# Second layer's X of blocks 1 to 4 transposed by VectorE instead of TensorE, with the orders of an opening, a late head pair and the last slots altered

## The chip, the cores and the metric

One Trainium2 chip, of which the kernel uses one core. The metric is the time of one execution in microseconds (us) of device time, as the median of several runs. A profile of one execution gives the span from its first to its last instruction, the instructions of each engine and the transfers of the DMA queues.

## The reference, cut to what matters

Three stages in fp32, one feeding the next. The shapes are fixed.

```
q, k, v : (4, 8, 576, 64)    f : (4, 8, 576)
attn = softmax(q k^T / 8 + decay(f), causal) v      # 32 heads, 576 tokens each
x = attn as (2304, 512)                             # tokens x model width

logits = x w_gate + modality_bias[modality_id]      # 8 experts, top 1
for each expert e:                                  # w1[e] 512 x 1024, w2[e] 1024 x 512
    y[tokens of e] = gate * (relu(x w1[e]) w2[e])

h = y w_in                                          # "second layer": 512 x 2048
out = max(0.01 h, h) w_out                          # 2048 x 512
```

## The kernel before, in words

TensorE is the engine that nearly everything goes through. Each fp32 product is made of three products of fp32r halves (high x high, high x low, low x high), so every operand is split by ScalarE (high half) and VectorE (low half) ahead of its matmuls.

**Attention** (0 to about 205 us) goes over 16 pairs of heads, g = 0 to 15. Its order on all five engines is written out by hand (`ordered(tc, MS)`): `first(g)`, `last(g)`, `third(g)`, `fourth(g)`. The operands of a pair are made ahead of it. `load(g)` brings the raw q and k (576 KB, 64 partitions of q over 64 of k). `prep_hi(g)`, called in `fourth(g - 2)`, makes the high half `aq` on VectorE (L386), brings three small row sets from `agd` (L390, L391) and copies the high half of k from partitions 64 to 127 to `bk` by a DMA (L393). `prep_lo(g)`, called in `first(g - 1)`, makes the low half (L403) and moves three more half tiles between partitions by DMAs (`bq`, `ak`, and `aq` onto itself at L406, which may start only when the copy at L393 has read its source). All these DMAs are issued by SyncE (SP), whose instructions go in order, and run on one queue. In `fourth(g)` the order before is `load(g + 3)`, `vload(g + 1)`, `prep_hi(g + 2)`.

The first pair has its q and k loaded twice, onto both partition halves (`qk0`), so that it needs no copies between partitions; pair 1 goes through `load`, `prep_hi`, `prep_lo` like the rest. Matmuls of no use, `warm(n)`, fill TensorE's first waits.

**Experts** (about 205 to 459 us). The tokens are put in slots of 128, each of one expert. `step(t)` runs slot t: first product `gemm1`, transposes `trh`, second product `gemm2` of the slot before, splits of the weights of the next slot (`split`), and the output `yout`, which scales by the gate (ScalarE, L1091) and scatters the rows to `yd` in DRAM (GpSimd). 18 steps always run; each further one stands in a branch on the number of slots (20 steps run with these inputs), and after the last comes `tail`, which ends the last slot and transposes X of block 0. Order by hand on all engines in `step`, on three in `tail`.

**Second layer** (about 459 us to the end). The 2304 tokens are cut into five blocks, four of 512 and one of 256. For each group of four of the 16 hidden blocks fb, and each token block b, `visit` runs `g1(b, fb)`: 12 matmuls into `u`, whose result goes ScalarE, VectorE, ScalarE, VectorE (L1303 to L1307) into the halves `gh`, `gl`; and `g2` of the visit before: 12 matmuls per 512 tokens. X of block b + 1 has to stand in SBUF, transposed to 128 features x 4 x 512 tokens in two halves, before `g1(b + 1, 0)`. `xload(b + 1)` is called at the first visit of block b and brings four tiles of 128 tokens (rows of 2052 bytes, the last word being the token's number). `xts` transposes a tile by four TensorE transposes into PSUM (L989), from which ScalarE makes the high and VectorE the low half (L993, L994). GpSimd copies the token numbers to `tid` (L985). Up to the first visit of block 1 TensorE's order is that of the program; after it the scheduler orders all engines by a simulated timeline. SP's first load of block 1 has to wait until the last scatter to `yd` has landed.

Of the kernel before, what the change touches and what calls it, by code (L numbers as in the profile page):

```python
# [19 lines left out]
P = 128  # L20
# [56 lines left out]
def fused(ctx: ExitStack, tc, qk0, qk2, vp, f, mid, wg, mb, w1, w2, w_in, w_out, out):  # L77
# [146 lines left out]
    with tc.tile_pool(name="pst", bufs=PST, space=PSUM) as pst:  # L224
# [15 lines left out]
        def gload(i):  # L240
            if i == 0:
                nc.sync.dma_start(wgs, wg.rearrange("(k p) e -> p k e", p=P))
                return
            nc.sync.dma_start(mbs.rearrange("p m e -> p (m e)"), mb.rearrange("(o m) e -> o (m e)", o=1).broadcast_to([P, 2 * E]))
            m32 = mid.bitcast(I32)
            for b in range(B):
                t0 = b * S
                nc.sync.dma_start(midi[:, b * NC:b * NC + 4, :], m32[t0:t0 + 4 * P, :].rearrange("(c p) t -> p c t", p=P))
            nc.sync.dma_start(midi[:64].rearrange("p (b c) t -> p b c t", c=NC)[:, :, 4, :], m32.rearrange("(b s) t -> s b t", b=B)[4 * P:])
# [23 lines left out]
        def load(g):  # L273
            if g == 1:

                xt[0] = pe.tile([P, NC, XW], F32, tag="x", name="x0")
                raw = xt[0].rearrange("p c d -> p (c d)")[:, :2 * S].rearrange("p (h s) -> p h s", h=2)
            else:
                raw = pe.tile([P, 2, S], F32, tag="raw", name=f"raw{g}", bufs=3)
            nc.sync.dma_start(raw, qk2[:, 2 * g:2 * g + 2, :])  # L280
            ops[g] = raw
# [21 lines left out]
        def start():  # L303
# [11 lines left out]
            load(1)  # L315
# [34 lines left out]
            load(2)  # L350
# [27 lines left out]
            nc.gpsimd.memset(midi, 0)  # L378
            ops[0] = (aq, bq, ak, bk)

        def prep_hi(g):
# [3 lines left out]
            bq, bk, a4, b4 = bqs[g % NBUF], bks[g % NBUF], aq4[g % NBUF], bq4[g % NBUF]  # L385
            nc.vector.tensor_scalar(aq, raw, qs, None, ALU.mult)  # L386
            if g == 1:
                nc.sync.dma_start(bk[0:64].bitcast(F32), h[64:128])
            for t, r0, c0 in ((bq, 64, 0), (bk, 66, 2)):
                nc.sync.dma_start(t[r0:r0 + 2].bitcast(F32), agd[c0:c0 + 2, 2 * g:2 * g + 2, :])  # L390
            nc.sync.dma_start(b4[64:66, :, :64].bitcast(F32), agd[0:2, 2 * g:2 * g + 2, 4 * P:])  # L391
            if g > 1:
                nc.sync.dma_start(bk[0:64].bitcast(F32), h[64:128])  # L393
# [526 lines left out]
        with ordered(tc, MS):  # L920
            start()
            prep_hi(1)
# [39 lines left out]
    xp = ctx.enter_context(tc.tile_pool(name="xp", bufs=4))  # L962
# [14 lines left out]
    def xts(b, sb, psums, part=None):  # L977
# [4 lines left out]
        for i in range(n // P) if part is None else part:  # L982
            r = XR[b, i]
            if t0 < FIX:
                nc.gpsimd.tensor_copy(tid[:, t0 // P + i:t0 // P + i + 1], r[:, DM:].bitcast(I32))  # L985
# [6 lines left out]
            c = slice(i * P, (i + 1) * P)  # L992
# [54 lines left out]
    with tc.tile_pool(name="rt2", reuse_waits="tile", bufs=1) as rt2, \  # L1047
# [16 lines left out]

        def keepg(t):
# [12 lines left out]
        def gemm2(t, k0, k1):  # L1078
            if k0 == 0:
# [345 lines left out]
```

## Time and profile before

| | |
|---|---|
| median of 3 runs | 864.98 us (864.28 to 865.23) |
| time of the profiled execution | 865.08 us |
| its span, first to last instruction | 863.4 us |
| TensorE busy, share of the span | 853.7 us, 99% |
| VectorE, ScalarE, GpSimd busy | 589.8, 503.3, 198.1 us |
| mean granted clock of TensorE | 0.996 of full speed |

The busy time of an engine is the sum of what its instructions cover. With one engine at 99%, a saving counts where that engine's work is removed or where it waits; what the other engines do counts where TensorE would have to wait for it. Times in the trace are us from the span's start.

### The profile page before, as it was taken

To read this page: it belongs to the slowest core of one execution; us is meant where nothing else is said; L and a number is where in the kernel's file an instruction comes from. 1 tells how busy PE (TensorE), PEld (TensorE's weight loads), DVE (VectorE), ACT (ScalarE), POOL (GpSimd) and SP (SyncE) were. 2 spreads that over 40 slices of the span, in tenths; PEclk is the share of its full clock that TensorE was granted. 3 is DMA by queue.
4 is the path that set the end of the run, shared out by engine and by line. 5 is a ranking of instruction groups with operands and counts; after the bars stand their busy time and mean duration, and the time that the engine had idled before them with its cause. 6 is when DMAs were issued, how large, how long until landed. Compare 5 with 4: busy or idle time off the path is not lost.

```text
span 863.4 us, 14450 instructions
## 1 busy us (share of the span) xinstructions
PE 853.7 (99%) x4760; PEld 705.9 (82%) x4760; DVE 589.8 (68%) x983; ACT 503.3 (58%) x965; POOL 198.1 (23%) x305
## 2 busy tenths in 40 slices
PE   8999999999999999999999999999999999999998
PEld 5888888878888888888878888888888888888887
DVE  6688777777769999999975563386337943473334
ACT  5888878867368999999884544353223422242222
POOL 6102222341148354339721000000000000001111
PEclk8999999999999999999999999999999999999999
DMA  7676787886485154131223240042001300011111
GB/s 224 174 192 178 206 216 195 208 204 227 113 284 185 63 168 155 40 97 62 81 83 89 64 132 0 1 126 70 1 0 51 122 25 1 0 49 49 50 49 74
DMA packets 34359, 92.96 MB, mean 108 GB/s; under 512 B 8582, under 2 KB 9254, under 8 KB 34275
## 3 DMA queue, kind: packets, MB, share of 16 engines
q1 hardware_dynamic: 29618, 77.23, 31.8%
q0 software_dynamic: 4640, 14.71, 5.2%
q8 instruction: 40, 0.66, 0.3%
q14 instruction: 45, 0.36, 0.1%
q10 hardware_dynamic: 16, 0.00, 0.0%
HBM read 132.09 MB, written 14.99 MB: 170 GB/s over the span
## 4 chain that ended last, share of the span: by engine, by line
PE 94%; DMA 2%; ACT 1%; DVE 1%; issue 1%; DVEq 0%; ACTq 0%; SPq 0%
PE u L1301 23%; PE a L1321 23%; PE h L215 13%; PE y L1083 13%; PE pv L527 5%; PE pt L515 4%; PE sc L426 2%; PE sc L427 2%; PE th L1073 2%; PE xo L551 1%; DMA bk<-aq 1%; PE tx L203 1%; PE pt L505 1%; PE sc L480 1%; PE sc L478 1%; PE fx L989 1%
## 5 line engine op out<-in xcount | busy, mean ns | idle before, releaser
L1303 ACT COPY us<-u 128x512 f32<-128x512 f32 (+1 forms) x80 | 43.4, 543 | 165.4 <-PE u L1301 165.1
L1304 DVE SCALAR_TENSOR_TENSOR us<-u,us 128x512 f32<-128x512 f32 (+1 forms) x80 | 51.0, 637 | 125.7 <-ACT us L1303 125.2
L1301 PE MATMUL u<-fxl,whii 128*128 128x512 f32 (+1 forms) x320 | 117.6, 369 | 0.0
L1301 PE MATMUL u<-fxh,whii 128*128 128x512 f32 (+1 forms) x320 | 117.5, 370 | 0.0
L1301 PE MATMUL u<-fxh,wloi 128*128 128x512 f32 (+1 forms) x320 | 117.5, 369 | 0.0
L1321 PE MATMUL a<-whio,gh 128*128 128x512 f32 x280 | 109.5, 391 | 0.0
L1321 PE MATMUL a<-wloo,gh 128*128 128x512 f32 x280 | 109.3, 390 | 0.0
L1321 PE MATMUL a<-whio,gl 128*128 128x512 f32 x280 | 104.7, 389 | 0.0
L177 DVE TENSOR_TENSOR w1l<-w1r,w1h 128x1024 fp32r<-128x1024 f32 x72 | 87.2, 1235 | 11.6 <-ACT w1h L173 11.6
L1334 POOL DMA_INDIRECT out<-acc,tid x16 | 15.8, 986 | 336.0 <-DVE acc L1328 299.1
L177 DVE TENSOR_TENSOR w2l<-w2r,w2h 128x1024 fp32r<-128x1024 f32 x68 | 80.2, 1222 | 1.3 <-ACT w2h L173 1.1
L441 ACT ACTIVATE p<-sc,nm 128x128 f32<-128x128 f32 (+3 forms) x128 | 66.1, 526 | 22.2 <-DVE nm L436 20.2
L1306 ACT CAST gh<-us 128x512 fp32r<-128x512 f32 (+1 forms) x76 | 44.6, 587 | 52.6 <-DVE us L1304 43.4
L173 ACT CAST w1h<-w1r 128x1024 fp32r<-128x1024 f32 x72 | 73.8, 1055 | 0.8 <-PE h L215 0.8
L1307 DVE TENSOR_TENSOR gl<-us,gh 128x512 fp32r<-128x512 f32 (+1 forms) x76 | 49.3, 648 | 36.1 <-ACT gh L1306 35.5
L173 ACT CAST w2h<-w2r 128x1024 fp32r<-128x1024 f32 x68 | 69.5, 1052 | 2.4 <-PE y L1083 2.0
L436 DVE TENSOR_REDUCE nm<-sc 128x2 f32<-128x256 f32 (+1 forms) x64 | 51.1, 820 | 27.1 <-PE sc L432 21.0
L1301 PEld LDWEIGHTS u<-fxh,wloi 128*128 128x128 f32 x320 | 60.3, 188 | 10.4
L1301 PEld LDWEIGHTS u<-fxh,whii 128*128 128x128 f32 x320 | 60.3, 188 | 10.1
L1301 PEld LDWEIGHTS u<-fxl,whii 128*128 128x128 f32 x320 | 60.3, 188 | 10.1
L166 POOL DMA_INDIRECT xg<-xs,gidx x22 | 58.5, 2657 | 36.9 <-PE xo L551 13.2
L1083 PE MATMUL y<-w2h,hh 128*128 128x512 f32 x160 | 64.6, 404 | 1.2 <-ACT hh L1075 1.2
(337 smaller groups left out, 1871.5 us busy)
## 6 DMA issues: line engine op xcount, KB each, us to landing
w1r<-w SPq DMA_DIRECT2D x88, 512.0 KB
w2r<-w SPq DMA_DIRECT2D x82, 512.0 KB
rwi<-w_in SPq DMA_DIRECT2D x16, 512.0 KB
rwo<-w_out SPq DMA_DIRECT2D x16, 512.0 KB
raw<-qk SPq DMA_DIRECT2D x14, 576.0 KB
vt<-vp SPq DMA_DIRECT2D x16, 320.0 KB
xr<-yd SPq DMA_DIRECT2D x18, 256.5 KB
bk<-aq SPq DMA_DIRECT2D x15, 288.0 KB
```

Source lines behind the costliest of these rows:

```text
L166: nc.gpsimd.indirect_dma_start(out=xg[t % 2], out_offset=None, in_=xs[:n, :], in_offset=bass.IndirectOffsetOnAxis(ap=m[:, i:i + 1], axis=0 ...
L173: nc.scalar.copy(hi, raw)
L177: nc.vector.tensor_tensor(lo, raw, hi.bitcast(F32), ALU.subtract)
L215: nc.tensor.matmul(Hp[t][:, n, :], lhsT=xp[t % 2][:, k * P:(k + 1) * P], rhs=wp[k][:, n * 512:(n + 1) * 512], start=(k == 0 and i == 0), s ...
L436: nc.vector.tensor_reduce(nm, view, axis=AX.X, op=ALU.max, negate=True)
L441: st["exp"] = nc.scalar.activation(pt[:, j, :], view[:, j, :], AF.Exp, bias=nm[:, j:j + 1], scale=1.0, accum_out=sms[g % 3][:, c, j:j + 1])
L1083: nc.tensor.matmul(Yp[t], lhsT=ap[:, k * P:(k + 1) * P], rhs=wp[k // 2][:, k % 2, :], start=(k == 0 and i == 0), stop=(k == NFB - 1 and i ...
L1301: nc.tensor.matmul(ps, lhsT=w[:, k * P:(k + 1) * P], rhs=x[:, k, :], start=(i == 0), stop=(i == 3 * NKB - 1))
L1304: nc.vector.scalar_tensor_tensor(us, ps, 0.01, us, ALU.mult, ALU.max)
L1306: nc.scalar.copy(gh, us)
L1307: nc.vector.tensor_sub(gl, us, gh.bitcast(F32))
L1321: nc.tensor.matmul(A[b][i], lhsT=x[:, c], rhs=w, start=(first and m == 0), stop=(last and m == 2))
```

## The change

1. **X of blocks 1 to 4.** `xload` brings a block with four DMAs, one for each quarter of the features, of 32 partitions each: partition 32 j + i holds, for quarter j, the tokens i, 32 + i, 64 + i, ..., in pieces of 512 bytes. One VectorE transpose in 32x32 blocks for each tile of 128 tokens (128x512 fp32, read in steps of 16 bytes) then gives the tile with features on the partitions; ScalarE and VectorE split it from SBUF. TensorE has no part in it. The order of the features becomes 4 p + k for partition p, which the host's layout of `w_in` follows; block 0, still on TensorE, reads its tile in steps of 16 bytes for that. All four tiles are in one buffer. The token numbers come by a DMA of their own. The tiles of blocks 2 to 4 move from visits 0, 0, 1, 2 to visits 2, 2, 3, 3 of the block before, ahead of `g1` in the program.
2. **Late pair.** In `fourth(g)`, `load(g + 3)` comes after `vload(g + 1)` and `prep_hi(g + 2)`.
3. **Opening.** Pair 1 is loaded like pair 0, onto both halves, k first, q in the place of `load(2)`. Its operands are made by `second(0)` to `second(2)` with one copy between partitions instead of four. `warm(4)` is put before the first transposes. `wgs` and `midi` are laid out on the host and come by one DMA each.
4. **Slots.** From slot 17 on, `yout(t - 2)` runs at the start of `step(t)` (or `tail`) instead of `yout(t - 1)` at the end, and `split(t, 0, 3)` at the start of `step(t)` instead of in `step(t - 1)`. The second product has one fixed PSUM tile.

```diff
 def load(g):
-    if g == 1:
-        xt[0] = pe.tile([P, NC, XW], F32, tag="x", name="x0")
-        raw = xt[0]...[:, :2 * S]
 def start():
-            load(1)
+            xt[0] = pe.tile([P, NC, XW], F32, tag="x", name="x0")
+            qr1, kr1 = (...[:, i * 2 * S:(i + 1) * 2 * S] ... for i in range(2))
+            nc.sync.dma_start(kr1, qk0[:, 1, 2:4, :])
...
-            load(2)
+            nc.sync.dma_start(qr1, qk0[:, 0, 2:4, :])
+def second(step):
+    if not step:
+        ...
+        nc.scalar.copy(ak, kr1)
+        nc.sync.dma_start(bks[1][0:64].bitcast(F32), ak[0:64].bitcast(F32))
+        operand_rows(1)
+        nc.vector.tensor_sub(ak[64:128], kr1[64:128], ak[64:128].bitcast(F32))
+        ...
+    if step == 1:
+        nc.vector.tensor_scalar(aq, qr1, 0.125, None, ALU.mult)
+        for r in (0, 64):
+            nc.gpsimd.tensor_copy(aq4[1][r:r + 64, :, :64], aq[0:64, :, 4 * P:].bitcast(F32))
+        return
+    nc.vector.scalar_tensor_tensor(bqs[1][0:64], qr1[0:64], 0.125, aq[0:64].bitcast(F32), ALU.mult, ALU.subtract)
+    nc.gpsimd.tensor_copy(bq4[1][0:64, :, :64], bqs[1][0:64, :, 4 * P:].bitcast(F32))
 def first(g):
-            if g + 1 < NG:
+            if 0 < g < NG - 1:
                 prep_lo(g + 1)
+            if not g:
+                second(1)
 def third(g):
+            if not g:
+                second(2)
...
+            if not g:
+                warm(4)
 def fourth(g):
-            if g + 3 < NG:
-                load(g + 3)
             if g + 1 < NG:
                 vload(g + 1)
             if g + 2 < NG:
                 prep_hi(g + 2)
+            if g + 3 < NG:
+                load(g + 3)
...
             start()
-            prep_hi(1)
+            second(0)
+            load(2)
 def xload(b):
-        for i in range(n // P):
-            XR[b, i] = xp.tile([P, XW], F32, tag="xr", name=f"xr{b}_{i}")
-            nc.sync.dma_start(XR[b, i], yd[t0 + i * P:t0 + (i + 1) * P, :])
+        r = xp.tile([P, 4, XW], F32, tag="xr", name=f"xr{b}")          # block 0: as before, in slices of r
+        XR[b] = r.rearrange("p c d -> p (c d)")[:, :n * 4]
+        for j in range(4):
+            nc.sync.dma_start(XR[b][32 * j:32 * j + 32].rearrange("b (q c) -> b q c", c=P), yd[t0:t0 + n, j * P:(j + 1) * P].rearrange("(q b) c -> b q c", b=32))
+        if t0 < FIX:
+            nc.sync.dma_start(tid[...].unsqueeze(2), yd[t0:t0 + n, DM:]...)
 def xts(b, sb, psums, part=None):
+            if b:
+                t = XQ[0].tile([P, 512], F32, tag="xq", name=f"xq{b}_{i}")
+                nc.vector.transpose(t.rearrange("p (i k c) -> p i k c", i=4, k=NKB), XR[b][:, i * 512:(i + 1) * 512].rearrange("p (i c k) -> p i k c", i=4, k=NKB))
+                t = t.rearrange("p (i k c) -> p k i c", i=4, c=32)
+                ...
+                nc.scalar.copy(h, t)
+                nc.vector.tensor_sub(l, t, h.bitcast(F32))
+                continue
+            rk = r[:, :DM].rearrange("p (c k) -> p k c", k=NKB)
             for k in range(NKB):
-                nc.tensor.transpose(ps[:, k * P:(k + 1) * P], r[:, k * P:(k + 1) * P], ident)
+                nc.tensor.transpose(ps[:, k * P:(k + 1) * P], rk[:, k], ident)
+        LATE = NSTAT - 1
 def tail(t):
+                if t >= LATE:
+                    yout(t - 1)
                 trh(t)
 def step(t):
+            if t > LATE:
+                yout(t - 2)
...
             keepg(t)
+            if t > LATE:
+                split(t, 0, 3)
...
-            if nx and t:
+            if nx and 0 < t < LATE:
                 split(t + 1, 0, 3)
...
-            if t:
+            if 0 < t < LATE:
                 yout(t - 1)
 def visit(v):
-                for k, i in (((2, 0), (2, 1), (3, 2), (3, 3)) if b == 0 else ((0, 0), (0, 1), (1, 2), (2, 3))):
+                for k, i in ((2, 0), (2, 1), (3, 2), (3, 3)):
...
-            for i in sorted(parts)[:1 if v <= GS else 2]:
+            for i in sorted(parts):
                 parts.pop(i)()
 host:
-    wi = ...reshape(NKB, P, NGB, P).transpose(1, 2, 0, 3)...
+    wi = ...reshape(P, NKB, NGB, P).transpose(0, 2, 1, 3)...
```

## Rows read from the trace of the kernel before

**Rows 1.** The page's first part: engine, busy us, share of the span, instructions.

```profile
PE 853.7 (99%) x4760; PEld 705.9 (82%) x4760; DVE 589.8 (68%) x983; ACT 503.3 (58%) x965; POOL 198.1 (23%) x305
```

**Rows 2.** Waits of TensorE: instruction waiting, releaser, us in total, times, longest.

```profile
PE sc L426 <- DMA aq<-aq: 1.6, 1, 1.6
PE y L1083 <- ACT hh L1075: 1.2, 1, 1.2
...
PE pt L515 <- ACT p L441: 0.8, 1, 0.8
PE sc L426 <- DVE ak L358: 0.8, 1, 0.8
```

**Rows 3.** Groups of TensorE by line, 467 to 535 us: the transposes of X.

```profile
L989 PE MATMUL fx<-ident,xr 128*128 128x128 f32 x56 | 8.4, 272 | 0.0
```

**Rows 4.** Chain that ended last, 440 to 560 us: start, us, what.

```profile
467.58 0.44 PE fx L989 x4
...
480.90 5.95 PE u L1301 x26
...
534.78 0.44 PE fx L989 x4
```

**Rows 5.** Groups of VectorE by line and shape: count, busy us, mean ns.

```profile
L1304 DVE SCALAR_TENSOR_TENSOR us<-u,us 128x512 f32<-128x512 f32 x64 | 44.2, 691 | 113.7 <-ACT us L1303 113.4
...
L675 DVE TENSOR_REDUCE lgs<-lp 128x40 f32<-128x320 f32 x1 | 0.8, 787 | 0.1
...
L754 DVE TENSOR_REDUCE stk<-ustk 128x20 f32<-128x160 f32 x1 | 0.3, 320 | 0.0
```

**Rows 6.** Timeline of SP's queue, 463 to 468 us: loads of block 1.

```profile
464.59 1.81 SPq L970 DMA_DIRECT2D xr<-yd  x4
```

**Rows 7.** Timeline of GpSimd, 463 to 468 us: first reader of those loads.

```profile
467.38 0.20 POOL L985 COPY tid<-xr 128x1 int32<-128x1 int32 x1 [5.44 <-DMA xr<-yd]
```

**Rows 8.** Windows: length, busy by engine, clock, DMA share, GB/s (last column).

```profile
15.60:17.00 1.40, 1.40 (x7) 1.40 (x7) 0.00 (x0) 1.40 (x6) 0.48 (x2) 0.50 1.06 204
...
466.00:470.40 4.40, 4.40 (x22) 3.51 (x21) 1.54 (x3) 1.21 (x2) 0.75 (x4) 1.00 0.92 285
...
480.90:505.10 24.20, 24.20 (x115) 19.96 (x115) 16.61 (x29) 13.46 (x23) 2.23 (x4) 1.00 0.38 108
```

**Rows 9.** Chain that ended last, 156 to 176 us.

```profile
161.43 9.20 DMA bk<-aq
...
170.68 3.54 DMA aq<-aq
```

**Rows 10.** Windows of the same stretch, columns as above.

```profile
159.00:170.00 11.00, 11.00 (x101) 9.38 (x100) 9.58 (x23) 9.14 (x28) 4.35 (x12) 1.00 0.97 212
...
170.50:171.50 1.00, 1.00 (x11) 0.88 (x10) 0.47 (x1) 0.31 (x2) 0.84 (x5) 1.00 0.18 60
```

**Rows 11.** Chain that ended last, 445 to 461 us.

```profile
447.85 1.76 ACT w2h L173 x2
...
449.63 0.70 ACT ys L1091
450.33 1.70 issue
...
452.16 0.59 ACT hh L1075
```

**Rows 12.** Windows of the opening, columns as above (PEclk is the third last).

```profile
13.00:14.00 1.00, 0.19 (x1) 0.18 (x1) 1.00 (x2) 0.70 (x4) 0.94 (x3) 0.88 0.96 207
14.00:20.60 6.60, 6.60 (x26) 5.14 (x26) 2.78 (x4) 3.89 (x15) 2.02 (x7) 0.50 0.81 172
```

**Rows 13.** Timeline of VectorE, 10 to 14 us.

```profile
10.93 0.82 DVE L386 TENSOR_SCALAR aq<-x,qs 128x1152 fp32r<-128x1152 f32 x1
12.16 1.02 DVE L436 TENSOR_REDUCE nm<-sc 128x2 f32<-128x256 f32 x2 [0.41 <-PE sc L429]
13.10 1.41 DVE L403 SCALAR_TENSOR_TENSOR x<-x,qs,aq 128x1152 fp32r<-128x1152 f32 x1
```

More of the change, by code (lines that the diff above doesn't have):

```diff
@@ L273, in load @@
         def load(g):
[L274 to L279 removed]
+            raw = pe.tile([P, 2, S], F32, tag="raw", name=f"raw{g}", bufs=3)
             nc.sync.dma_start(raw, qk2[:, 2 * g:2 * g + 2, :])
@@ L377, in start, with operand_rows @@
                 nc.gpsimd.memset(t[:, S:], 0.0)
-            nc.gpsimd.memset(midi, 0)
             ops[0] = (aq, bq, ak, bk)
+            ops[1] = (qr1, kr1)
+        def second(step):
+            if not step:
+                qr1, kr1 = ops[1]
+                aq, ak = (aqk.tile([P, 2, S], F32R, tag=n, name=f"{n}1") for n in ("aq", "ak"))
+                nc.scalar.copy(ak, kr1)
+                nc.sync.dma_start(bks[1][0:64].bitcast(F32), ak[0:64].bitcast(F32))
+                operand_rows(1)
+                nc.vector.tensor_sub(ak[64:128], kr1[64:128], ak[64:128].bitcast(F32))
+                st["second"] = qr1, aq
+                ops[1] = (aq, bqs[1], ak, bks[1])
+                return
+            qr1, aq = st["second"]
+            if step == 1:
+                nc.vector.tensor_scalar(aq, qr1, 0.125, None, ALU.mult)
+                for r in (0, 64):
+                    nc.gpsimd.tensor_copy(aq4[1][r:r + 64, :, :64], aq[0:64, :, 4 * P:].bitcast(F32))
+                return
+            nc.vector.scalar_tensor_tensor(bqs[1][0:64], qr1[0:64], 0.125, aq[0:64].bitcast(F32), ALU.mult, ALU.subtract)
+            nc.gpsimd.tensor_copy(bq4[1][0:64, :, :64], bqs[1][0:64, :, 4 * P:].bitcast(F32))
+        def operand_rows(g):
+            for t, r0, c0 in ((bqs[g % NBUF], 64, 0), (bks[g % NBUF], 66, 2)):
+                nc.sync.dma_start(t[r0:r0 + 2].bitcast(F32), agd[c0:c0 + 2, 2 * g:2 * g + 2, :])
+            nc.sync.dma_start(bq4[g % NBUF][64:66, :, :64].bitcast(F32), agd[0:2, 2 * g:2 * g + 2, 4 * P:])
         def prep_hi(g):
@@ L384, in prep_hi @@
             h = aq.bitcast(F32)
-            bq, bk, a4, b4 = bqs[g % NBUF], bks[g % NBUF], aq4[g % NBUF], bq4[g % NBUF]
+            bk, a4 = bks[g % NBUF], aq4[g % NBUF]
             nc.vector.tensor_scalar(aq, raw, qs, None, ALU.mult)
[L387 to L393, printed above, removed]
+            operand_rows(g)
+            nc.sync.dma_start(bk[0:64].bitcast(F32), h[64:128])
             for r in (0, 64):
@@ L967, in xload @@
         t0, n = blocks[b]
-        for i in range(n // P):
-            XR[b, i] = xp.tile([P, XW], F32, tag="xr", name=f"xr{b}_{i}")
-            nc.sync.dma_start(XR[b, i], yd[t0 + i * P:t0 + (i + 1) * P, :])
+        r = xp.tile([P, 4, XW], F32, tag="xr", name=f"xr{b}")
+        if not b:
+            for i in range(n // P):
+                XR[b, i] = r[:, i, :]
+                nc.sync.dma_start(XR[b, i], yd[t0 + i * P:t0 + (i + 1) * P, :])
+            return
+        XR[b] = r.rearrange("p c d -> p (c d)")[:, :n * 4]
+        for j in range(4):
+            nc.sync.dma_start(XR[b][32 * j:32 * j + 32].rearrange("b (q c) -> b q c", c=P), yd[t0:t0 + n, j * P:(j + 1) * P].rearrange("(q b) c -> b q c", b=32))
+        if t0 < FIX:
+            nc.sync.dma_start(tid[:, t0 // P:(t0 + n) // P].unsqueeze(2), yd[t0:t0 + n, DM:].bitcast(I32).rearrange("(c p) o -> p c o", p=P))
     X = {}
@@ L1063, in fused @@
         gc = mw.tile([P, 2], F32, name="gc")
+        yp = pmy.tile([P, 512], F32, name="yp")
         def keepg(t):
@@ L1078, in gemm2 @@
         def gemm2(t, k0, k1):
-            if k0 == 0:
-                Yp[t] = pmy.tile([P, 512], F32, tag="y", name=f"y{t}")
             for k in range(k0, k1):
                 for i, (ap, wp) in enumerate(((hh, w2h), (hh, w2l), (hl, w2h))):
-                    nc.tensor.matmul(Yp[t], lhsT=ap[:, k * P:(k + 1) * P], rhs=wp[k // 2][:, k % 2, :], start=(k == 0 and i == 0), stop=(k == NFB - 1 and i == 2))
-        Yp = {}
+                    nc.tensor.matmul(yp, lhsT=ap[:, k * P:(k + 1) * P], rhs=wp[k // 2][:, k % 2, :], start=(k == 0 and i == 0), stop=(k == NFB - 1 and i == 2))
         def yout(t):
@@ L1281, in fused @@
          tc.tile_pool(name="fz", reuse_waits="tile", bufs=1) as fz, \
+         tc.tile_pool(name="xq", reuse_waits="tile", bufs=2) as xq, \
          tc.tile_pool(name="pfa", reuse_waits="tile", bufs=1, space=PSUM) as pfa, \
@@ L1286, in fused @@
             wset(fx, i)
+        XQ.append(xq)
         G = {}
@@ L1400 @@
     w2 = inputs["moe_w2"].reshape(E, NFB, P, DM).transpose(0, 2, 1, 3).reshape(E, P, NFB * DM)
-    wi = inputs["moe2_w_in"].reshape(NKB, P, NGB, P).transpose(1, 2, 0, 3).reshape(P, NGB, NKB * P)
+    wi = inputs["moe2_w_in"].reshape(P, NKB, NGB, P).transpose(0, 2, 1, 3).reshape(P, NGB, NKB * P)
     arrays = {
-        "qk0": np.stack([np.concatenate([t, t], axis=0) for t in (qk2[:D, :2], qk2[D:, :2])], axis=1),
+        "qk0": np.stack([np.concatenate([t, t], axis=0) for t in (qk2[:D, :4], qk2[D:, :4])], axis=1),
         "qk2": qk2,
```

24 lines of the change are left out of this document (11 added, 13 removed).

## The prediction

> **What bounds the kernel now.** I read the page's first part first: TensorE is busy for 853.7 of 863.4 us [rows 1], so a gain has to be TensorE work removed or a TensorE wait closed, and a loss a new TensorE wait. Its list of waits holds four that the change touches, 4.4 us together: 1.6 for a copy of `aq`, 1.2 for `hh`, 0.8 for `p`, 0.8 for `ak` [rows 2]. The reader should see that the waits are few and single (each occurs once). Then I took the groups of TensorE in the stretch of the X transposes (56 of them, four for each of 14 tiles) [rows 3], the chain there for what a tile costs [rows 4], VectorE's groups for the price of the new work [rows 5], the queues that feed it [rows 6, 7] with windows for rates and load [rows 8], and one view for each wait [rows 9 to 13]. A difference within 0.2% (1.7 us) counts as no change: about what a measurement of this kernel can tell.
>
> **The sum's base.** The profiled execution took 865.08 us (span 863.4, 1.7 around it), 0.1 above the median of the runs shown. I sum against 865.1 and take 0.1 off at the end.
>
> **X, what leaves TensorE.** A row of four transposes takes 0.44 us of the chain [rows 4], the first and the last of 14, though each is listed with 272 ns [rows 3], since they overlap. 14 x 0.44 = 6.1 us. TensorE waits for nothing there and the transposes lie between its products, so all of it comes off: -6.1.
>
> **X, what VectorE gets.** 14 transposes of 128x512 fp32. No transpose by VectorE is in the trace. An operation of the same size that reads in sequence takes 0.69 us L1304 in [rows 5]. The change reads with a step of 16 bytes. The nearest row is the reduction L675, whose reads are 32 or 64 bytes apart: 320 elements in 787 ns, while the reduction L754 does 160 neighbouring ones in 320 ns. With about 153 ns fixed (691 less 512 at 1.05; 320 less 160 at 1.04 gives the same), L675 pays 1.98 ns an element, nearly double. So a transpose lies between 0.69 and 512 x 1.98 + 153 = 1.17 us; I take 1.17, the row with spread reads being nearest.
>
> The Trainium skill (SBUF — State Buffer, section Door 1: The DMA port swizzle) says that reads which change to another 16-byte line at every access pay for it, with no figure; by that the 0.69 is out, and the sum with 0.69 would be about 2 us lower. L675 agrees at 32 bytes, no row shows 16.
>
> **Block 1, the place where time goes back.** Its load starts when the last scatter has landed, at 464.6 [rows 6]. Before, the first tile (256.5 KB) had a reader at 467.38 [rows 7], 2.8 us later; at 285 GB/s [rows 8], 466.0 to 470.4 0.9 of that is transfer, 1.9 fixed. A VectorE transpose needs all four DMAs, since each brings 32 of the 128 partitions: 1.05 MB, 3.7 us at 285 GB/s, 5.1 at 204, the rate while copies to 64 partitions run [rows 8], 15.6 to 17.0. With so few partitions at a time I take 5.1: the data is there at 471.6 (470.2 at best). VectorE, in order, then has four transposes (4.7), four low halves at 0.69 (2.8), and between them three steps of visits 2 and 3 (2.1): 9.5 us, so X stands at 481.1. TensorE needs it for u(1,0), now at 480.9 [rows 4], but five groups of 0.44 vanish ahead of it: 478.7. A wait of 2.4 us, on an engine that had none. Behind it stand g2(0,3) and all after. Best: loads at 470.2 and transposes at 0.69 (7.6 us) end at 477.8, no wait. Worst: the two further VectorE steps of those visits are ordered ahead too and one more 0.7 is lost to waiting for ScalarE's high halves: +4.5. I take +2.4.
>
> **Blocks 2 to 4.** Here the load has a visit or more to spare: one buffer means that it waits for the transposes of the block before, but it is issued about 20 us ahead of need. What is tight is VectorE while block 1 is multiplied, when weights 4 and 5 of the second layer are split too: 16.6 busy of 24.2 us [rows 8], 480.9 to 505.1. Four transposes add 4.7, the stretch loses 1.8: 21.3 of 22.4. It fits, barely; +0.5, between 0 and +2.4 (half of what is added turns up as waits). The token DMA (512 words per block) and GpSimd's 12 copies less are hidden: GpSimd is busy 23% [rows 1], and the numbers are needed at the output. On SP's queue only weight loads stand behind the new five DMAs per block, not needed until the second group of hidden blocks.
>
> **Late pair.** The chain: copy of `bk` 9.2 us, then `aq` 3.54, then TensorE [rows 9]. The queue ran at 0.97 share until 170, so the copy of `bk` was long because the load of pair 15 (576 KB) and others stood in front of it. With the load behind, `bk` lands 590 KB / 212 GB/s = 2.8 us earlier, and the copy of `aq`, which waits for it on SP, is issued earlier. The bytes ahead of `aq` are the same either way, so only the hole counts: 0.18 share from 170.5 to 171.5 and the ramp around it [rows 10], some 1.5 us. The move puts a vload and prep_hi's four DMAs ahead of the load on SP; the load then also waits for VectorE's `aq`, with only the low-half copies and stores behind it, and is needed a pair later. So 1.5 of the 1.6 us go: -1.5 (0 if the queue stays full instead, -1.6 at most).
>
> **Slots.** At `tail` ScalarE goes `w2h` twice, `ys`, 1.7 us in which it waits for nothing shown (the branch), then `hh` at 452.16 [rows 11]; TensorE waits 1.2 for it [rows 2]. The change puts `ys` behind the branch, still ahead of `hh`, which moves nothing; what helps is the one `w1h` split that no longer stands ahead of the two `w2h` (0.9 by [rows 11], half of it eaten by an earlier wait for TensorE): -0.5, at best the 1.2. The splits put at the start of slots 18 and 19 are needed only for the last quarter of `gemm1`. Against it, block 0's 16 transposes now read with 16-byte steps; at double they cost 1.8, 0.7 of it hidden in the rest of the wait: +0.6 in all as the upper end.
>
> **Opening.** At 13 to 14 us TensorE is busy for 0.19 us, waiting for `p`; then the granted clock is 0.5 (1.2 GHz) from 14.0 to 20.6, TensorE busy throughout [rows 12]. `warm(4)` fills that wait. If the clock stays at 2.4 GHz, the 6.6 us become 3.3; I take 1.0 back, because ScalarE and VectorE then set the pace for a pair: -2.3. Costs inside: ahead of the maxima at 12.16 VectorE gets a 1152-wide subtraction (1.41 by L403) in the place of 0.82 [rows 13], which ends at 12.34, 0.2 late; ScalarE's 1152-wide copy of k now stands ahead of the first exponentials, which wait for those maxima, so it is covered as long as k lands in time, as the same bytes did for L386 at 10.93. L403's 1.41 moves behind the next maxima. SP issues one copy between partitions for pair 1 instead of four, and the load of q stands where that of pair 2 stood, which moves back behind it. Ends: -3.3, and +0.3 if the clock falls anyway.
>
> **Sum.** -6.1 + 2.4 + 0.5 - 1.5 - 0.5 - 2.3 = -7.5: 857.6 against the profile, 857.5 for the median. All low ends: -12.2, 852.8. All high ends: +1.7, 866.7.
>
> **Rivals.**
> - *All is covered* (0.25): the load of block 1 or the transposes are quicker than taken, no wait at u(1,0), and the clock gives its full 3.3: -6.1 - 1.5 - 0.5 - 3.3 = -11.4, 853.6. For it: VectorE may begin tile by tile as soon as the load is there; against it: L675.
> - *The clock falls anyway* (0.15): the wait for `ak` before it stays [rows 2], and the opening gives nothing: 857.5 + 2.3 = 859.8, up to 862 with a longer wait at block 1.
> - *The late pair does not do what it says* (0.06): as the same bytes stand ahead of `aq`, the queue stays full and the wait stays: 859.0.
> - *VectorE's order becomes the bound, slower* (0.07): a transpose placed ahead of the steps that make `gl` holds them while its load is under way, at every block. The gains other than X's wait are 6.1 + 1.5 + 0.5 + 2.3 = 10.4, so it decides from 2.6 us for each of four blocks; at 3.5 (three steps of 1.17 each) it is 865.0 - 10.4 + 14 = 868.6. For it: [rows 8] leave 1 us of VectorE free in 22 at block 1; against: blocks 2 to 4 have time to spare. The Trainium skill (VectorE: DVE Perf Modes, section Rules for kernel authors) sends 128x128 transposes to TensorE where PSUM will do as a target; by that rule this rival would be the case. The trace bears it out only where VectorE is full, and TensorE at 99% speaks against it.
> - *No change* (0.05): the same in smaller size, 8.7 to 12.1 us of waits.
>
> **How the numbers follow.** The forecast's own case (855.5 to 859.5) has 0.42. Range 852.7 to 862.5: it takes in the covered case and the clock's, and leaves out the slower ones and the tails. Faster 0.42 + 0.25 + 0.15 + 0.06 = 0.88, same 0.05, slower 0.07.
>
> **What the profile after would show.** L989 with 16 transposes instead of 72; a VectorE transpose group x14, mean near 1170 ns (690 would prove the rival); a TensorE wait of about 2.4 us for `fxl` at the first product of block 1; none for `aq` near 172; one for `hh` of 0.7; clock 1.0 from 14 us on. The prediction is wrong if TensorE waits in blocks 2 to 4, if the clock is still 0.5 after 14 us, or if block 1's load takes far from 7 us.

## The result

The changed kernel takes 869.61 us (median of 6 runs, 869.04 to 870.52), the kernel before beside it 865.11 (6 runs, 864.28 to 866.33). The ratio is 1.0051, 95% interval 1.0040 to 1.0061: slower by half a per cent, where 857.5 was forecast. What came is the forecast's rival "VectorE's order becomes the bound", priced at 868.6 with a chance of 0.07.

The first part of the page after, beside [rows 1]:

```profile
PE 848.9 (98%) x4708; PEld 700.2 (81%) x4708; DVE 601.7 (69%) x997; ACT 502.2 (58%) x964; POOL 193.5 (22%) x292
```

TensorE is busy for 4.8 us less, and the span (868.6 us) is 5.2 longer. So it waits some 10 us more. Its list of waits in the kernel after, where [rows 2] stood before:

```profile
PE a L1366 <- ACT gh L1351: 5.9, 2, 5.0
PE a L1366 <- ACT acc L1371: 2.6, 1, 2.6
PE sc L439 <- ACT p L454: 1.3, 1, 1.3
...
PE a L1366 <- DVE gl L1352: 0.9, 1, 0.9
PE yp L1120 <- DVE hl L1115: 0.9, 1, 0.9
PE sc L439 <- DVE ak L351: 0.8, 1, 0.8
```

The wait for `aq` is gone in this profile, that for `hh` has become one of 0.9 for `hl`, and 9.4 us stand in products `a` of the second layer, which waited for nothing before. The place of the loss is fixed by the first product of the second layer, in the timeline of TensorE, before and after:

```profile
459.19 1.08 PE L1301 MATMUL u<-fxh,whii 128*128 128x512 f32 x4
```

```profile
456.81 1.08 PE L1346 MATMUL u<-fxh,whii 128*128 128x512 f32 x4
```

From there to the end of the span the kernel before takes 863.4 - 459.19 = 404.2 us, the changed one 868.6 - 456.81 = 411.8. All that precedes it is 2.4 us quicker; the second layer is 7.6 slower although 6.1 us of transposes have left it. So 13.7 us were added there. Windows of the kernel after (length, busy time by engine, granted clock third last):

```profile
467.00:475.00 8.00, 2.14 (x7) 0.91 (x5) 5.42 (x8) 2.37 (x4) 0.00 (x0) 0.78 0.12 7
475.00:480.00 5.00, 4.97 (x15) 4.00 (x16) 3.54 (x5) 1.78 (x4) 0.00 (x0) 0.66 0.63 121
...
495.00:505.00 10.00, 7.37 (x27) 5.67 (x26) 8.01 (x12) 5.92 (x11) 0.00 (x0) 0.83 0.23 41
505.00:540.00 35.00, 33.99 (x150) 27.48 (x149) 22.07 (x37) 15.37 (x28) 0.00 (x0) 1.00 0.23 69
```

```profile
471.40:473.40 2.00, 0.50 (x1) 0.50 (x2) 2.00 (x5) 1.19 (x2) 0.00 (x0) 0.53 0.00 0
473.40:478.20 4.80, 3.89 (x10) 2.49 (x9) 4.45 (x6) 1.93 (x4) 0.00 (x0) 0.50 0.21 50
...
498.70:502.10 3.40, 2.88 (x7) 2.30 (x8) 3.37 (x6) 3.04 (x6) 0.00 (x0) 0.52 0.00 0
```

TensorE is idle for 5.9 us of 467 to 480, 2.6 of 495 to 505 and 1.0 after: 9.5. After the two long waits the clock is at half (1.2 GHz); the products in those stretches (0.50 + 3.89 and 2.88 us busy) would take half the time at 2.4: 2.2 and 1.4 us. Waits and clock make 13.1 of the 13.7; where the other 0.6 went isn't shown.

The chain that ended last, kernel after, shows what ended the waits (start, us, what):

```profile
462.54 6.91 DMA xr<-yd
...
474.98 1.02 DVE xq L1015
476.01 0.32 SPq L997
...
477.44 5.77 DMA xr<-yd
483.23 0.05 DVEq L1015
483.33 2.07 DVE xq L1015 x2
...
491.19 5.68 DMA xr<-yd
496.95 2.05 DVE xq L1015 x2
...
504.02 4.10 DMA xr<-yd
```

Before, this stretch of the chain was TensorE's own [rows 4]. Now it is a ring: load, four transposes, buffer free, next load. The timeline of VectorE tells why TensorE feels it (in brackets the idle time before, and what ended it):

```profile
461.79 0.69 DVE L1352 TENSOR_TENSOR gl<-us,gh 128x512 fp32r<-128x512 f32 x1 [0.69 <-ACT gh L1351]
469.57 2.05 DVE L1015 STREAM_TRANSPOSE xq<-xr 128x512 f32<-128x512 f32 x2 [7.09 <-DMA xr<-yd]
471.55 0.65 DVE L1349 SCALAR_TENSOR_TENSOR us<-u,us 128x512 f32<-128x512 f32 x1
...
483.33 2.07 DVE L1015 STREAM_TRANSPOSE xq<-xr 128x512 f32<-128x512 f32 x2 [3.99 <-DMA xr<-yd]
...
496.95 2.05 DVE L1015 STREAM_TRANSPOSE xq<-xr 128x512 f32<-128x512 f32 x2 [3.84 <-DMA xr<-yd]
...
508.24 2.06 DVE L1015 STREAM_TRANSPOSE xq<-xr 128x512 f32<-128x512 f32 x2 [1.33 <-DMA xr<-yd]
```

At 462.5 VectorE comes to block 1's transposes and stands there for 7.09 us, idle, until the rows land at 469.5. Behind them in its queue is `us` of the second visit, which then runs at once, at 471.55. `gh` follows, and TensorE, without `gh`, has nothing to do from 467.9. The program has block 1's tiles in the third and fourth visit; the scheduler, which orders VectorE here by its own simulated timeline, put the first two in front of the `us` of the second. The transposes of blocks 2 to 4 were moved forward in the same way: block 2's, which the program has in the seventh and eighth visit, begin at 483.33, in front of the `us` of the fourth. That the scheduler took each load to be done by then is a guess; no run shows what it assumed.

The wait of 2.6 for `acc` has the same cause one engine further on. ScalarE's timeline, kernel after:

```profile
498.06 0.62 ACT L1018 CAST fxh<-xq 128x512 fp32r<-128x512 f32 x1 [4.71 <-DVE xq L1015]
498.59 0.58 ACT L1371 COPY acc<-a 128x512 f32<-128x512 f32 x1
```

ScalarE stands idle for 4.71 us in front of the high half of block 3's first tile, which has to wait for VectorE's transpose and so for the load. Behind it in ScalarE's queue is `acc`, the copy that frees an accumulator of TensorE; the products that it copies had ended by 491.8.

### The profile page after: what moved, and what is told of

The parts are those of the page before. It is cut to its first block, busy times and chain, and to the rows that moved or that the text cites. A ratio compares the mean times of both kernels' runs of the same rounds, so it can differ in the third digit from the quotient of the medians.

```text
span 868.6 us, 14296 instructions
## 1 busy us (share of the span) xinstructions
PE 848.9 (98%) x4708; PEld 700.2 (81%) x4708; DVE 601.7 (69%) x997; ACT 502.2 (58%) x964; POOL 193.5 (22%) x292
## 4 chain that ended last, share of the span: by engine, by line
PE 90%; DMA 3%; DVE 3%; issue 1%; ACT 1%; POOL 1%; SPq 1%; DVEq 0%; POOLq 0%; ACTq 0%
PE a L1366 21%; PE u L1346 20%; PE h L215 13%; PE yp L1120 12%; PE pv L540 5%; PE pt L528 4%; DMA xr<-yd 3%; PE sc L439 3%; PE sc L440 2%; PE th L1112 2%; PE xo L564 1%; DVE xq L1015 1%; PE pt L518 1%; PE tx L203 1%; PE sc L493 1%
## 5 line engine op out<-in xcount | busy, mean ns | idle before, releaser
L1366 PEld LDWEIGHTS a<-whio,gh 128*128 128x128 f32 x280 | 53.4, 191 | 20.8 <-ACT gh L1351 7.3
L1346 PEld LDWEIGHTS u<-fxl,whii 128*128 128x128 f32 x320 | 60.3, 188 | 10.4
L1120 PE MATMUL yp<-w2h,hh 128*128 128x512 f32 x160 | 64.6, 404 | 0.0
```

The costliest lines, as they stand in the source:

```text
L1120: nc.tensor.matmul(yp, lhsT=ap[:, k * P:(k + 1) * P], rhs=wp[k // 2][:, k % 2, :], start=(k == 0 and i == 0), stop=(k == NFB - 1 and i == 2))
L1346: nc.tensor.matmul(ps, lhsT=w[:, k * P:(k + 1) * P], rhs=x[:, k, :], start=(i == 0), stop=(i == 3 * NKB - 1))
L1366: nc.tensor.matmul(A[b][i], lhsT=x[:, c], rhs=w, start=(first and m == 0), stop=(last and m == 2))
```

## The experiments

They were run in three groups, e1 to e4 and e5 to e8 on one chip and e9 to e12 on another, with the kernel before beside each group (its medians there: 866.18, 866.22 and 865.84 us). What precedes the second layer varies by up to 2.7 us between profiles of kernels that have it in common, so X is judged by the second layer: from its first product to the end of the span, in one profile each. The four profiles with X on TensorE (before, e1, e7, e8) give 404.2 to 404.9 for it, so differences below about 0.7 us say nothing. Waits are those of 0.4 us and more, from the layer's first product to 560 us.

| kernel | us | ratio to before (95%) | first product | second layer | waits of TensorE |
|---|---|---|---|---|---|
| changed kernel | 869.61 | 1.0051 (1.0040 to 1.0061) | 456.81 | 411.8 | 9.4 |
| e1 X on TensorE | 863.27 | 0.9961 (0.9943 to 0.9980) | 456.45 | 404.4 | 0 |
| e2 X alone | 873.61 | 1.0077 (1.0053 to 1.0100) | 463.10 | 410.5 | 7.2 |
| e3 no ring | 867.25 | 1.0019 (1.0005 to 1.0033) | 458.70 | 407.9 | 6.8 |
| e4 data there | 862.59 | 0.9965 (0.9949 to 0.9980) | 459.18 | 399.7 | 1.8 |
| e5 block 1 on TensorE | 863.94 | 0.9975 (0.9958 to 0.9992) | 457.10 | 404.1 | 3.5 |
| e6 behind low halves | 861.15 | 0.9941 (0.9922 to 0.9961) | 458.50 | 400.9 | 1.6 |
| e7 no products in the gap | 865.41 | 0.9991 (0.9968 to 1.0013) | 457.54 | 404.6 | 0 |
| e8 late load back | 863.06 | 0.9973 (0.9951 to 0.9995) | 458.01 | 404.9 | 0 |
| e9 e5, tiles spaced | 860.22 | 0.9921 (0.9899 to 0.9943) | 458.26 | 399.7 | 0 |
| e10 X alone, behind low halves | 862.85 | 0.9965 (0.9948 to 0.9982) | 460.13 | 401.1 | 1.7 |
| e11 blocks 2 to 4 behind | 867.67 | 1.0019 (1.0004 to 1.0034) | 457.71 | 408.0 | 6.9 |
| e12 e6, weights moved | 859.86 | 0.9923 (0.9902 to 0.9944) | 458.13 | 400.5 | 1.2 |

**Which part loses: e1 and e2.** e1 is the changed kernel with the old `xload`, `xts`, places of tiles and layout of `w_in`; e2 is the kernel before with the new ones. Of the diff between the kernels, e1 takes back, and e2 alone makes:

```diff
-xp = tc.tile_pool(name="xp", bufs=4)
+xp = tc.tile_pool(name="xp", bufs=1)
...
-                nc.tensor.transpose(ps[:, k * P:(k + 1) * P], r[:, k * P:(k + 1) * P], ident)
+                nc.vector.transpose(t..., XR[b][:, i * 512:(i + 1) * 512]...)
...
-for k, i in (((2, 0), (2, 1), (3, 2), (3, 3)) if b == 0 else ((0, 0), (0, 1), (1, 2), (2, 3))):
+for k, i in ((2, 0), (2, 1), (3, 2), (3, 3)):
```

> The changed kernel with X of blocks 1 to 4 put back on TensorE (old loads, old layout of w_in, old places of the tiles); opening, late pair and slots stay changed. Theory 1 (the X part alone loses, the other three edits gain the 2.4 us by which the second layer starts earlier in the changed kernel's trace): 865.1 - 2.4 = 862.7, between 862.0 and 863.3, no TensorE wait for the second layer's rows, clock 1.00 from 460 to 540. Theory 2 (the loss lies in the other edits, and the 2.4 us are lost again by what they do to the queues): 865 or above. Theory 3 (the forecast's sizes for the other edits, -4.3): 860.8.

> The kernel before with the X part alone (loads, transposes by VectorE, w_in layout, places of the tiles). Theory 1 (X costs what stands between the two kernels plus what the other edits gain): 865.1 + 4.5 + 2.4 = 872.0, between 871 and 873, with the same three TensorE waits at blocks 1, 2 and 3 of about 9 us together and two dips of the clock. Theory 2 (the other edits lose): 860 or below, since 6.1 us of TensorE's transposes are gone.

The first theory holds in both: the X part alone costs 6.7 us of 866.2 (1.0077), the other three edits gain 3.4 (0.9961; 1.7 to 4.9). With X on TensorE the second layer takes 404.4 (404.2 before) without a wait, with the new X 410.5. In its details e2 missed: 873.61 is above the 871 to 873, and its profile has two waits in place of three, 4.2 for `gl` and 3.0 for `acc`, each with the half clock behind it.

**Work or waiting: e4.** The transposes read a weight tile that stands in SBUF, so that nobody waits for the loaded rows.

```diff
-nc.vector.transpose(t..., XR[b][:, i * 512:(i + 1) * 512]...)
+nc.vector.transpose(t..., W[i, 0][0].bitcast(F32)...)
```

> The changed kernel with the 14 transposes of blocks 1 to 4 reading a weight tile that has been in SBUF since the first layer, in place of the loaded rows; the loads still run, but nobody waits for them (so the second layer's input of blocks 1 to 4 is other data). VectorE's work is the same 14 transposes of the same shape. Theory 1 (the loss is the waiting for rows at the head of VectorE's queue, with the clock that falls after it): TensorE has no wait over 1 us between 457 and 540, the clock stays at 1.00, and the 6.1 us of transposes are a gain: 869.6 - 9.5 - 4 = 856, between 855 and 858. Rival (the transposes' work crowds VectorE): 866 or above, with TensorE waits for the low halves. Forecast's term for that crowding (+0.5 in blocks 2 to 4, up to 2.4): 856.5 to 858.5.

Its waits of TensorE between 455 and 560 us:

```profile
PE a L1366 <- DVE gl L1352: 1.4, 1, 1.4
PE a L1366 <- ACT gh L1351: 0.4, 1, 0.4
```

The same fourteen transposes, and the second layer takes 399.7: 4.7 less than on TensorE, 12.1 less than in the changed kernel. The work on VectorE isn't what costs; waiting for rows is. The scheduler gave the transposes other places too (the last ends at 484.9, in the changed kernel at 510.3), so e4 doesn't part the order from the buffer; the next three do. One wait of 1.4 passed the 1 us expected. The time of 856 was missed by 6.6 us (862.6): the first product came 2.4 later than in the changed kernel's profile (459.18), and the layer took 1.4 more than the sum has (399.7 for 398.3); the rest isn't placed.

**The buffer or the order: e3, e6, e11.** e3 gives each block's rows a space of their own (that of its later accumulator); e6 keeps the one buffer and puts VectorE's work on X behind the last `gl` before it; e11 does so for blocks 2 to 4 only.

```diff
 # e3
-        XR[b] = r.rearrange("p c d -> p (c d)")[:, :n * 4]
+        r = ROWS[b] = XQ[1].tile([P, n * 4], F32, name=f"rows{b}")
+        XR[b] = r
...
-                        Y[b, i] = fx.tile([P, DM], F32, name=f"acc{b}_{i}")
+                        Y[b, i] = ROWS[b][:, i * DM:(i + 1) * DM] if b else fx.tile([P, DM], F32, name=f"acc{b}_{i}")
 # e6
-            nc.vector.tensor_sub(gl, us, gh.bitcast(F32))
+            G["last"] = nc.vector.tensor_sub(gl, us, gh.bitcast(F32))
...
-            for i in sorted(parts):
-                parts.pop(i)()
+            if parts:
+                with tc.issue_after(G["last"].ins):
+                    for i in sorted(parts):
+                        parts.pop(i)()
             g1(b, fb)
 # e11, against e6
-                with tc.issue_after(G["last"].ins):
+                with tc.issue_after(G["last"].ins) if b else nullcontext():
```

> The changed kernel with the rows of blocks 1 to 4 loaded each into the space that later holds that block's accumulator, so no load waits for the transposes of the block before; nothing else is changed by hand. Theory 1a (VectorE, in order, stands before a transpose whose rows are not there; the single buffer makes this happen three more times after block 1): the waits at blocks 2 and 3 go, 3.6 us of TensorE waits and the second dip (1.7), the wait at block 1 stays: 869.6 - 5.3 = 864.3, between 863 and 866. Theory 1b (the single buffer is not what matters, only where the transposes stand in VectorE's order): 868 or above. Rival (it is the transposes' own work on VectorE that crowds out the steps of the visits): unchanged, 869 to 870.

> The changed kernel with one edit: VectorE's transposes, and the low halves made from them, are queued behind the last low half of the visit before them; block 1 stays on VectorE, the single buffer stays. Theory 1a (the order on VectorE is the cause, not the single buffer): the waits of blocks 2 and 3 (3.6 us and 1.7 of the clock) are gone; block 1 keeps a wait, since its rows land at about 469.5 and four transposes with four low halves take 7.5 us from there while TensorE wants them at 475: a wait for gh of about 2.4 and one for the rows of about 2, in place of 5.9. The second layer takes 404 to 407 from its first product (411.8 in the changed kernel), the kernel 0.996 to 1.000 of the kernel before. Theory 1b (the single buffer by itself): no change at blocks 2 and 3, 411 or more.

> The changed kernel with the transposes of blocks 2 to 4 queued behind the low half of the visit before, those of block 1 left where they are. Theory 1 by the ledger of the changed kernel's trace (block 1: 5.9 us of waits and 2.2 of clock, blocks 2 and 3: 3.6 and 1.7): the second layer takes 400.9 + 7.1 = 408, between 406.5 and 408.5, with the wait for gh of about 5 and the dip of the clock after it; 0.999 to 1.003 of the kernel before. Rival (block 1's wait comes from the blocks behind it): 403 or less.

e3, the chain and VectorE's timeline:

```profile
464.36 7.88 DMA rows<-yd
```

```profile
472.37 2.06 DVE L1017 STREAM_TRANSPOSE xq<-rows 128x512 f32<-128x512 f32 x2 [8.00 <-DMA rows<-yd]
```

Blocks 2 and 3 wait no more, but all the loads now leave at once and block 1's takes 7.88 us instead of 6.91, so VectorE stands still for 8.00 and the layer gains 3.9 instead of 5.3; the time, 867.25, missed the 863 to 866. In e6, with the buffer as it was, VectorE's timeline:

```profile
464.77 0.69 DVE L1349 SCALAR_TENSOR_TENSOR us<-u,us 128x512 f32<-128x512 f32 x1 [0.60 <-ACT us L1348]
466.15 0.69 DVE L1352 TENSOR_TENSOR gl<-us,gh 128x512 fp32r<-128x512 f32 x1 [0.69 <-ACT gh L1351]
471.13 2.08 DVE L1015 STREAM_TRANSPOSE xq<-xr 128x512 f32<-128x512 f32 x2 [4.29 <-DMA xr<-yd]
...
491.29 2.07 DVE L1015 STREAM_TRANSPOSE xq<-xr 128x512 f32<-128x512 f32 x2
...
498.25 2.07 DVE L1015 STREAM_TRANSPOSE xq<-xr 128x512 f32<-128x512 f32 x2
```

and its waits of TensorE, 455 to 560 us:

```profile
PE a L1366 <- ACT gh L1351: 0.9, 1, 0.9
PE u L1346 <- DVE us L1349: 0.7, 1, 0.7
```

The reader should see `us` and `gl` of the second visit now in front, and block 2's transposes at 491 and 498 with no idle time before them: their rows were there. The kernel is faster than the changed one and than e3 (0.9941), by the order alone: the edit names VectorE's, and the scheduler planned the other engines around it, so that `acc` waits no more either. It beats the 404 to 407 expected: block 1 was reckoned at two waits of 2.4 and 2 us, and had one of 0.9. What is left may be ScalarE's queue, which no run parts from the rest: ScalarE stands idle for 6.19 us in front of the high half at 472.31, while the `us` behind it had its products from 469.6. e11 keeps block 1's 5.0 for `gh`, and the half clock behind it, as these rows of its windows and waits say:

```profile
475.00:480.00 5.00, 4.16 (x10) 3.29 (x11) 4.20 (x7) 2.34 (x4) 0.00 (x0) 0.50 0.40 93
```

```profile
PE a L1366 <- ACT gh L1351: 5.0, 1, 5.0
PE a L1366 <- DVE gl L1352: 1.2, 1, 1.2
```

It takes 408.0, as reckoned: block 1 is worth 408.0 - 400.9 = 7.1 us, blocks 2 to 4 the other 411.8 - 408.0 = 3.8. For blocks 2 to 4 either remedy ends the waits, a space of their own (e3) or the order (e11); for block 1, whose load waits for no other, only the order does.

**X in the right order without the other edits: e10.** The kernel before with e2's and e6's edits.

> The kernel before with the X part alone and VectorE's work on X queued behind the low half of the visit before. Theory 1 (the order on VectorE is all that was wrong with the X part): the second layer takes 400 to 402 from its first product (404.2 in the kernel before, 410.5 with the X part alone in its given order), the kernel 865.1 - 3.3 = 861.8, 0.996 of the kernel before. Rival (the X part needs the earlier start that the other edits give): 404 or more, 1.000 or above.

0.9965 and 401.1: the X part gains 3 us by itself when placed so, where it loses 6.7 in its given order.

**Looking for the best: e5, e9, e12.** e5 puts block 1 back on TensorE (loaded tile by tile, with a second buffer for the rows) and the rest behind the low halves; e9 takes one of the two tiles of a visit behind `g1` again; e12 is e6 with other visits for the split of weights 4 and 5.

```diff
 # e5, with e6's edit
-            if b:
+            if b > 1:
                 t = XQ[0].tile([P, 512], F32, tag="xq", ...)
                 nc.vector.transpose(...)
 # e9, against e5
+                if parts and not b:
+                    parts.pop(min(parts))()
 # e12, against e6
-                if GS <= v < GS + 2 * (NSET - GS):
-                    for _ in wpart(*divmod(GS + v, 2)):
+                if v in (8, 9, 12, 13):
+                    for _ in wpart(4 + (v > 9), v % 2):
```

> The changed kernel with two edits: block 1 is transposed by TensorE from rows loaded tile by tile, as block 0 is; and VectorE's work on X of blocks 2 to 4 is queued behind the last low half of the visit before it, so that no transpose stands ahead of a step whose data come sooner. (The rows of blocks 1, 2 and 4 go into the space of a later accumulator, block 3's into the old buffer.) Theory 1 (waiting for rows at the head of VectorE's queue is the whole loss): no TensorE wait over 0.5 us and no dip of the clock in the second layer; it takes 404.4 (as with X on TensorE) - 10 x 0.44 = 400.0 from its first product to the end, and the kernel 4.4 us less than with X on TensorE, 0.991 of the kernel before. Rival (the transposes' work on VectorE delays the steps of the visits, block 1's weights being split then): 402 or more, 0.994 or above.

> The kernel with block 1 transposed by TensorE and blocks 2 to 4 by VectorE behind the low halves, but with the first of the two tiles of a visit of block 0 transposed before its first product and the second after it, as in the kernel before. Theory 1 (the 2.8 us that TensorE waited for low halves of X there come from two tiles in a row through one PSUM buffer): that wait is gone, the second layer takes 404.1 - 2.8 = 401.3 from its first product, 0.993 to 0.995 of the kernel before. Rival (TensorE waits there for the loads of rows, which more transfers share): 403 or more.

> The kernel with VectorE's work on X of all four blocks behind the low halves, and the split of the second layer's weights 4 and 5 moved from the four visits of block 1 to the first two visits of blocks 2 and 3, in which no transpose falls. Theory (VectorE, busy throughout from 495 to 505, causes the 0.8 us that TensorE still waits for us near 503): this wait goes, the second layer takes 400.1 from its first product, the kernel 0.993 of the kernel before. Rival (that wait is for the rows' transposes alone): 400.9 as without the move.

e5 missed, by a fault of the edit. Its waits of TensorE, 455 to 560 us:

```profile
PE fx L1033 <- DVE fxl L1037: 2.8, 2, 1.4
PE u L1352 <- DVE us L1355: 0.7, 1, 0.7
```

Two tiles in a row go through one PSUM tile, and the second waits 1.4 for the low half of the first. With the spacing of the kernel before (e9) TensorE has no wait at all there, and the layer takes 399.7. That is less than the 401.3 expected of e9, and what e5 should have given: 404.4 less ten tiles of 0.44 is 400.0. e12 lost the wait for `us` and has 1.2 for `gh` in place of 0.9; its 400.5 and e6's 400.9 can't be told apart, so the crowding of VectorE at 495 to 505 costs nothing that these profiles could show. e9 and e12 are the best two, 5.6 and 6.0 us below the kernel before.

**The other edits: e7, e8.** Both are e1 less one edit: `warm(4)` left out; `load(g + 3)` first in `fourth` again.

```diff
 # e7
-            if not g:
-                warm(4)
 # e8
+            if g + 3 < NG:
+                load(g + 3)
             if g + 1 < NG:
                 vload(g + 1)
             if g + 2 < NG:
                 prep_hi(g + 2)
-            if g + 3 < NG:
-                load(g + 3)
```

> The kernel with X on TensorE and the other three edits, without the four products that fill the gap after the first scores (warm(4)). Theory 1 (it is these products that keep the clock up): the granted clock is 0.5 for some 6.6 us from about 14 us on, as in the kernel before; the opening then ends between 0.5 and 2.3 us later than with them. Rival (the other edits of the opening, loads and copies moved, keep TensorE fed): clock 1.00 from 14 to 20 without the products too. Theory 3 (ScalarE and VectorE set the pace there, so a slow clock costs little): the dip returns, and group 0 ends less than 0.5 us later.

> The kernel with X on TensorE and the other three edits, but for the load of a pair three ahead, which is put back in front of the loads of v and the low halves' copies as in the kernel before. Forecast's step (the move closes TensorE's wait for the copy of aq near 172): the wait of 1.6 us or so returns between 160 and 175, where the same kernel with the move had 0.2; the time 0.5 to 1.7 us higher. Rival (the copies late in the queue depend on its rate from run to run, not on the order): waits of the same size with and without the move.

e8's total can't be told from e1's (863.06 and 863.27): the late pair's move gains nothing that shows. e7's is 2.1 us above it. Windows of the opening in e10 (opening of before), e7 and e9:

```profile
14.00:21.00 7.00, 7.00 (x28) 5.36 (x27) 3.18 (x4) 4.29 (x16) 2.02 (x7) 0.54 0.81 186
```

```profile
14.00:21.00 7.00, 6.66 (x44) 5.04 (x44) 6.30 (x9) 6.41 (x21) 3.74 (x9) 1.00 0.37 131
```

```profile
14.00:21.00 7.00, 6.84 (x43) 5.62 (x41) 5.87 (x8) 6.00 (x19) 3.73 (x9) 0.85 0.46 144
```

All three profiles with the old opening have the half clock; of the eleven with the new one, two (e6, e9) have it for about 3.4 us, the others not, e7 without the four products among them. By that one profile the rival would be right, that the moved loads and copies are enough. The other runs say otherwise. The mean granted clock over a run is 0.998 to 1.000 in all twelve of e1, whose median is 863.27, and 0.992 to 0.997 in eight of the twelve of e7, whose median is 865.41; the profiled one has 0.999. (e8, which has the products and ran in e7's group, has 863.06, and 0.998 or more in nine of its twelve.) Without the four products the clock falls in most runs. At which place it falls isn't shown, since one run of e7 was profiled, but the two kernels differ in these products alone. So theory 1 is borne out, in the runs if not in the profile. Late pair, windows of e6 (load behind) and e8 (load in front):

```profile
160.00:175.00 15.00, 12.91 (x113) 10.74 (x113) 11.58 (x31) 11.90 (x33) 8.96 (x32) 1.00 0.98 217
```

```profile
160.00:175.00 15.00, 13.22 (x113) 11.06 (x113) 11.35 (x29) 10.90 (x30) 9.10 (x34) 0.98 0.92 211
```

TensorE waits for the copy of `aq` with either order: 2.09 and 1.78 us here; 0 to 2.09 in the ten profiles with the move (mean 1.0), 0.57 to 2.56 in the four without (mean 1.6). That the move closes the wait isn't shown.

## Why the prediction was wrong

- **Bound: right.** TensorE is busy for 98% of the span, and its waits decided.
- **X off TensorE, -6.1: right.** e9's ten tiles gave 4.7 (4.4 by the forecast's 0.44).
- **Price of a transpose, 1.17 us: right in kind, 0.09 too high.** The groups of VectorE and TensorE, kernel after:

```profile
L1015 DVE STREAM_TRANSPOSE xq<-xr 128x512 f32<-128x512 f32 x14 | 14.8, 1081 | 16.3 <-DMA xr<-yd 16.3
...
L1027 PE MATMUL fx<-ident,xr 128*128 128x128 f32 x16 | 2.3, 284 | 0.0
```

  It is 1081 ns; and the 16.3 us idle before them, all for the rows, tell the story in one row. Block 0's reads in 16-byte steps cost 284 against 272 ns [rows 3]: next to nothing. The Trainium skill (SBUF — State Buffer, section Door 1: The DMA port swizzle) has reads that change to another 16-byte line at each access pay. VectorE's 1081 ns against the 691 of `us` [rows 5] would fit, but no run parts the step from the transposing; TensorE's 284 against 272 hardly show it.
- **Block 1, +2.4: the step that failed.** The load took 8.5 us from its first issue at 461.02 to the first transpose at 469.57 (6.91 from the last of the four issues), where the forecast had 7.0 from the first: 1.5 short, but not what decided, since in e6 it takes as long (471.13 - 462.71 = 8.4) and TensorE's wait is 0.9. The forecast let VectorE do the visits' steps between the transposes and put the price at u(1,0), where TensorE has no wait at all. In the queue the transposes stood in front of a `us` that could have run 8.5 us earlier (in e6 it runs 464.77 - 458.50 = 6.3 us after the layer's first product, here 471.55 - 456.81 = 14.7); so the wait for the load, not only the work behind it, passed to TensorE, at the second visit. It measured 7.1 (e11 less e6), the clock in it.
- **Blocks 2 to 4, +0.5: failed for the same reason.** "Issued about 20 us ahead of need" held for the time at which X is needed, but not for VectorE, which stood idle before the transposes of blocks 2 and 3 for 3.99 and 3.84 us, as did ScalarE behind it (4.71, in front of `acc`); and the next load could only leave when they were done. It cost 3.8 us more than in e11. In all the X terms came to 411.8 - 404.4 + 6.1 = +13.5 where +2.9 was forecast, and 10.9 of it goes with the order. With the order set right (e6), X gives 404.4 - 400.9 = 3.5, close to the forecast's 6.1 - 2.9 = 3.2; but not by its mechanism, since the wait of 2.4 at u(1,0) isn't there either, and e6's 1.6 us of waits stand elsewhere.
- **Late pair, -1.5:** its wait is gone in the one profile after, but there, with 0.2 to 2.1, in the nine others with the same order; the means differ by 0.6, and e8, without the move, is no slower. The rival "does not do what it says" stands.
- **Slots, -0.5:** `hh` 1.2 became `hl` 0.9: 0.3, in one profile.
- **Opening, -2.3: right in kind.** The clock stays up mostly, and by e7's runs the four products that were to keep it up are worth about 2.1 us. The first pair's output (`xo`) starts at 30.98 in the changed kernel and 31.66 before; in the other profiles with the new opening at 29.4 to 30.1. So the opening itself ends 0.7 to 2.2 sooner. Late pair, slots and opening together gave 3.4 for 4.3. The whole account in the forecast's terms is -6.1 + 13.5 - 3.4 = +4.0, and the kernel is 4.5 slower.
- **The rival that came** had the mechanism: a transpose ahead of the visits' steps "holds them while its load is under way". Its 868.6 lies near the 869.6 partly by luck: it reckoned 3.5 us at every one of four blocks, 14 in all, where 7.1 fell on block 1 alone, and 10.4 of other gains, where 9.5 came. It was given 0.07 because blocks 2 to 4 "have time to spare". They had, and the scheduler put their transposes forward all the same, block 2's from the seventh visit to the fourth. The Trainium skill (VectorE: DVE Perf Modes, section Rules for kernel authors) would keep 128x128 transposes on TensorE. Here the loads do part of the transposing and VectorE only 32x32 blocks, so the rule's case isn't quite this one; e6, e9 and e10 show that in the right order VectorE's are worth 3 to 4.7 us.

## What to carry to other kernels

When work moves to an engine that goes in order, ask first what stands behind it in that queue and whether its input comes by a DMA; the cost is then not its busy time but the DMA's remaining time, paid by whoever waits for what stands behind. The same goes for the next engine's queue, if it has to take up the result. If a planner sets the order by assumed load times, tie the new work behind the steps whose data come sooner: here that one line turned +6.7 us into -3. Judge an edit by its own stage (here from the first product of the layer), since the stages ahead varied by up to 2.7 us from profile to profile. And where a profile shows one run, look at the clock and time of the others before it decides: e7's profile spoke against eight of its twelve runs.

## What the runs showed of the hardware

- TensorE's clock in the second layer was at half only in the profiles of the four kernels with a wait of 2.6 us or more there (changed kernel, e2, e3, e11), for 6.8 and 3.4 us in the changed kernel; with waits of 1.4 and less it stayed at 2.4 GHz.
- One block's load (1.05 MB in four DMAs to 32 partitions each) took 6.91 us from the last issue with only the loads of token numbers behind it, 7.88 with other blocks' loads behind it: 152 and 133 GB/s over the whole time, its fixed part included.
- Four DMAs of which each fills a quarter of the partitions make every reader wait for all four: GpSimd's first reader of a 128-partition tile came 2.8 us after the load's issue before [rows 6, 7], the first transpose 8.5 us after.
